# Second product of a squared-ReLU FFN with the token rows stationary, and an earlier first chunk

## The chip, the cores and the metric

The kernel runs on one core of a Trainium2 chip. The core has TensorE (PE: matrix products, with its weight loads shown apart as PEld), VectorE (DVE), ScalarE (ACT), GpSimd (POOL) and SyncE (SP, which here only issues DMAs). The metric is the device time of one execution in microseconds. The kernel before takes 222.59 us (median of three runs, 222.51 to 223.92).

## The reference

Attention with sketched quadratic features, and then a feed-forward layer with squared ReLU. Batch 4, 4 heads, 1088 positions of 32 numbers each, sketches of 8 rows, so 64 features; the FFN has width 128 and 2048 hidden units, and 4352 rows pass through it.

```python
def phi(x):
    a = np.einsum('rd,bhsd->bhsr', S1, x)
    b = np.einsum('rd,bhsd->bhsr', S2, x)
    return np.einsum('bhsi,bhsj->bhsij', a, b).reshape(*x.shape[:-1], r * r)
q_p, k_p = (phi(q), phi(k))
kv = np.einsum('bhsf,bhsd->bhfd', k_p, v)
z = np.sum(k_p, axis=2)
num = np.einsum('bhsf,bhfd->bhsd', q_p, kv)
den = np.einsum('bhsf,bhf->bhs', q_p, z)[..., None] + 1e-06
attn = num / den
x = attn.transpose(0, 2, 1, 3).reshape(B * S, H * D)
h = np.maximum(x @ w_in, 0.0)
out = h * h @ w_out
```

Inputs and output are float32.

## The kernel before

**Tiles.** The 1088 positions of a batch are 1024, cut into two groups of 512 (four tiles of 128 tokens), and a remainder of 64; the remainders of two batches share a tile of 128 rows. The FFN works on chunks: eight of 512 tokens (two per batch) and one of 256 that holds all remainders. The FFN's input `xT` of a chunk is float16, 128 features by the chunk's tokens, scaled per token by a factor that is undone at the end (`beta`).

**Attention.** For each batch `k_gen` makes the features of k: transposes on TensorE (`xt_ps`, L194), projections (`ab_ps`, L180), outer products (L221, by VectorE in the first batch and GpSimd later). `Kv` accumulates the products with v in PSUM (`kv_ps`, L249), and `finish` copies them to `kvbd` (L60). `q_gen` makes the features of q, transposes them (`t_ps`, L299) and calls `x_gen`: `numerators` writes `nd` (PSUM, two banks, one buffer), and `normalize` reads it with a chain of small VectorE instructions (L329 to L351), writes the scaled rows `xs` (L358, the last reader of `nd`), which TensorE transposes (`x_ps`, L370) and ScalarE copies to `xT` (L373). `normalize` is a generator with three yields, so that its caller can put other work in between.

**FFN.** A chunk has 16 blocks, one for each 128 hidden units. `first_product` multiplies the block's 128 columns of `w_in` (stationary, float16) with `xT` into `pg` (L516); ScalarE applies ReLU (`gt`, L519); VectorE squares (`g`, L520, float32). `block` adds the second product to `po` (L535), with 128 rows of `w_out` stationary and `g`'s 512 tokens moving, both float32. The first product is issued two blocks ahead (`LOOK = 2`). After 16 blocks `po` holds the output transposed: model features by tokens.

**Store.** `store_gen` copies `po` to `oT` (ScalarE, L482), transposes the four tiles of 128 tokens back on TensorE into `o_ps` (L487, a buffer of the `ms` ring), multiplies with `beta` on VectorE (`o_sb`, L493) and issues the output DMA on SP (L501). `po` has one buffer, so the next chunk's second product waits for the copy.

**Order.** The start (`start`) is laid out by hand, instruction by instruction: it makes k and the first q group of batch 0 and pushes the first chunk (`first`) and the second group's features (`second`) through. `idle_products` are float32 products of a zero tile that only keep TensorE occupied. After the start, `block` calls with attention pieces between them (`pump`, `lanes`) give the program order, and a scheduler then orders each engine's instructions.

**PSUM.** Eight banks: `ms` two, `pg` two, `po` one, `kv` one, `nd` two.

Of the kernel before, what the change touches and what calls it, by code (L numbers as in the profile page):

```python
# [8 lines left out]
F32 = mybir.dt.float32  # L9
# [3 lines left out]
def _v(t: bass.AP, off: int, free, p0: int = 0, n: int = 128):  # L13

    p = list(t.ap)[0]
    return bass.AP(
        t.tensor, t.offset + p0 * p[0] + off, [[p[0], n]] + [list(d) for d in free]
    )
# [3 lines left out]
def kernel(  # L22
# [11 lines left out]
    nc = tc.nc  # L34

    B, H, S, D = 4, 4, 1088, 32
    DFF, NC = 2048, 16
# [3 lines left out]
    VW = D + 1  # L41
# [10 lines left out]
    fpool = ctx.enter_context(tc.tile_pool(name="ffn", bufs=3))  # L52
    pspool = ctx.enter_context(
        tc.tile_pool(name="psm", bufs=2, space=bass.MemoryType.PSUM)
    )

    def evict(eng, dst, src):
        if eng is nc.scalar:
            return nc.scalar.copy(dst, src)  # L59
        return eng.tensor_copy(out=dst, in_=src)  # L60
# [59 lines left out]
    w_o = cpool.tile([128, DFF], F32)  # L120
# [12 lines left out]
    iden = cpool.tile([128, 128], F32)  # L133
# [14 lines left out]
        nc.vector.memset(_v(v_main[i], D, [[VW, H * NJ]]), 1.0)  # L148

    def idle_products(n):  # L150
        idle_ps = pspool.tile([128, 512], F32, name="idle_ps", tag="po", bufs=1)
        for i in range(n):
            nc.tensor.matmul(idle_ps[:, 0:128], zero[:, :], zero[:, :])

# [14 lines left out]
    def spread_vrem(r, eng, pin=False):  # L169
        ins = eng.tensor_copy(  # L170
            out=_v(v_rem[r], 0, [[VW, H], [1, D]]), in_=_v(v_rm[r], 0, [[D, H], [1, D]])
        )
        if pin:
            pinned(ins)
# [11 lines left out]

    def proj_t(src, g, T, eng, tag="ms"):


        n = 4 if T == 4 else 1  # L190
        w = NJ * D if T == 4 else E
        xt_ps = pspool.tile([128, 512], F32, tag=tag, bufs=2)
        for i in range(n):
            nc.tensor.transpose(  # L194
                xt_ps[:, 128 * i : 128 * i + 128],
                src[:, w * i + 128 * g : w * i + 128 * g + 128],
                iden[:, :],
            )
        xt = apool.tile([128, 512], F32, tag="xt", bufs=4)
        evict(eng, xt[:, 0 : 128 * n], xt_ps[:, 0 : 128 * n])  # L200
        return xt

    def proj(xt, T, tag, eng, outer, ps_tag="ms", m=32):

        n = 4 if T == 4 else 1
        ab_ps = pspool.tile([128, 256], F32, tag=ps_tag, bufs=2)
        for i in range(n):
            tiled(ab_ps, 64 * i, 64, xt, 128 * i, w_bd[:, :], m=m)
        ab = apool.tile([128, 256], F32, tag="ab", bufs=3)
        if T == 4:  # L210
            evict(
                eng,
                _v(ab, 0, [[16, 4], [64, 4], [1, 16]]),
                _v(ab_ps, 0, [[64, 4], [16, 4], [1, 16]]),
            )
        else:
            evict(eng, ab[:, 0:64], ab_ps[:, 0:64])
        ph = apool.tile([128, 1024], F32, tag=tag, bufs=3)
        for t0 in range(0, T, 2):
            m = min(2, T - t0)  # L220
            outer[(t0 // 2) % len(outer)].tensor_tensor(  # L221
                out=_v(ph, 256 * t0, [[64, 4 * m], [8, 8], [1, 8]]),
                in0=_v(ab, 64 * t0, [[16, 4 * m], [1, 8], [0, 8]]),
                in1=_v(ab, 64 * t0 + 8, [[16, 4 * m], [0, 8], [1, 8]]),
                op=mult,
            )
        return ph
# [9 lines left out]
    class Kv:  # L237
# [1 line left out]

        def __init__(self, b, m=32):
            self.b, self.m, self.started = b, m, set()
            self.ps = pspool.tile([128, 2 * VW], F32, name="kv_ps", tag="kv", bufs=1)

        def _add(self, ph, c0, vt, v0, p0, n, last):
            for pr in range(2):
# [47 lines left out]
    def feature_t(ph, T, pr, eng):  # L295

        t_ps = pspool.tile([128, 512], F32, tag="ms", bufs=2)
        for t in range(T):
            nc.tensor.transpose(  # L299
                t_ps[:, 128 * t : 128 * t + 128],  # L300
                ph[:, 256 * t + 128 * pr : 256 * t + 128 * pr + 128],
                iden[:, :],
            )
        sb = apool.tile([128, 512], F32, tag=f"phT{pr}")
        evict(eng, sb[:, 0 : 128 * T], t_ps[:, 0 : 128 * T])
        return sb
# [69 lines left out]
    chunks = []  # L376
# [5 lines left out]
    def x_gen(b, g, phT, m=32):  # L382
        nd = numerators(b, phT, m)
        yield 1
        xT = apool.tile([128, 512], F16, name="xT", tag="xT", bufs=3)
        beta = yield from normalize(nd, 4, xT, 0)
        chunk_of(b, g, xT, beta)
        yield 1

    def q_gen(b, g, outer, m=32):  # L390
        eng = nc.scalar
        xt = proj_t(q_sb[b], g, 4, eng)
        yield 1
        ph = proj(xt, 4, "ph_q", eng, outer, m=m)
        yield 3
        phT = []
        for pr in range(2):
            phT.append(feature_t(ph, 4, pr, eng))
            yield 1
        yield from x_gen(b, g, phT)  # L400
# [46 lines left out]
    now = [0]  # L447
    lanes = []
# [28 lines left out]
                except StopIteration:  # L477
                    lanes.remove(lane)

    def store_gen(po, nt, betas, dsts):  # L480
        oT = fpool.tile([128, 512], F32, tag="oT", bufs=2)
        nc.scalar.copy(oT[:, 0:nt], po[:, 0:nt])  # L482
        yield 1
        T = nt // 128
        o_ps = pspool.tile([128, 512], F32, tag="ms", bufs=2)
        for t in range(T):
            nc.tensor.transpose(  # L487
                o_ps[:, 128 * t : 128 * t + 128], oT[:, 128 * t : 128 * t + 128], iden[:, :]
            )
        o_sb = fpool.tile([128, 512], F32, tag="o_sb", bufs=2)  # L490
        t0 = 0
        for beta, n in betas:
            nc.vector.tensor_tensor(  # L493
                out=_v(o_sb, 128 * t0, [[128, n], [1, 128]]),
                in0=_v(o_ps, 128 * t0, [[128, n], [1, 128]]),
                in1=_v(beta, 0, [[1, n], [0, 128]]),
                op=mult,
            )
            t0 += n
        for dst, p0, n, c0, w in dsts:  # L500
            nc.sync.dma_start(dst, _v(o_sb, c0, [[1, w]], p0, n))  # L501
        yield 1

    LOOK = 2
    stream = []
# [21 lines left out]
    po = [None]  # L527

    def block():
        while len(stream) <= LOOK and first_product():  # L530
            pass
        ci, c, nt, g2 = stream.pop(0)
        if c == 0:
            po[0] = pspool.tile([128, 512], F32, name="po", tag="po", bufs=1)
        nc.tensor.matmul(  # L535
            po[0][:, 0:nt], w_o[:, 128 * c : 128 * c + 128], g2[:, 0:nt],
            start=(c == 0), stop=(c == NC - 1),
        )
        now[0] += 1
        if c == NC - 1:  # L540
            lanes.insert(0, [store_gen(po[0], nt, *chunks[ci][2:]), now[0]])


    dve, act, pool = nc.vector, nc.scalar, nc.gpsimd
# [1 line left out]
    def whole(gen):  # L546
        for _ in gen:
            pass


    def start():
        s_ps = pspool.tile([128, 16], F32, name="s_ps", tag="kv", bufs=1)
        xk = [proj_t(k_sb[0], 0, 4, act)]
        nc.tensor.transpose(s_ps[:, :], s_nat[:, :], iden[0:16, 0:16])
        for h in range(H):
            nc.vector.tensor_copy(
                out=_v(w_bd, 16 * h, [[1, 16]], 32 * h, 32),
                in_=_v(s_ps, 0, [[1, 16]], 32 * h, 32),
            )
        xk.append(proj_t(k_sb[0], 1, 4, act))  # L560
        idle_products(2)
        pk = [proj(x, 4, "ph_k", act, (dve,), "pg", m=64) for x in xk]
        idle_products(1)
        xq = proj_t(q_sb[0], 0, 4, act)
        spread_v(0, act, 0, 4)
        pq = proj(xq, 4, "ph_q", act, (dve,), "pg", m=64)
        xkr = proj_t(k_rm[0], 0, 1, act)
        spread_v(0, act, 4, 4, (0, 1))
        spread_v(0, pool, 4, 4, (2, 3))
        spread_vrem(0, pool)  # L570
        ph_krem[0] = proj(xkr, 1, "ph_kr", act, (dve,), "pg", m=64)
        kv0 = Kv(0, 64)
        kv0.tiles(pk[0], 0, range(4))
        pqT = [feature_t(pq, 4, 0, act)]
        kv0.tiles(pk[1], 1, range(4))
        pqT.append(feature_t(pq, 4, 1, act))
        kv0.finish((dve, dve))
        first = x_gen(0, 0, pqT, 64)
        next(first)
        for c in range(4):  # L580
            act.copy(
                w_in[:, 512 * c : 512 * c + 512], w_in32[:, 512 * c : 512 * c + 512]
            )
        second = q_gen(0, 1, (dve,), 64)
        next(second)
        next(first)
        next(first)
        next(second)
        idle_products(3)
        next(first)  # L590
        whole(first)
        return second

# [30 lines left out]
    for c in range(NC):  # L624
        block()
        pump(2)
# [31 lines left out]
```

## Time and profile before

| | us |
|---|---|
| median of three runs | 222.59 |
| the three runs | 222.51, 223.92, 222.59 |
| the profiled execution, whole | 223.71 |
| its span, first to last instruction | 221.9 |
| second product, PE busy (288 records) | 140.8 |
| first product, PE busy (128 records of 512 columns) | 48.2 |
| ReLU, ACT busy (144) | 81.9 |
| squaring, DVE busy (144) | 104.0 |
| `oT` copies, ACT busy (9) | 5.1 |
| `o_ps` transposes, PE busy (34) | 5.6 |

A row of the profile gives start and length in us, engine, source line, operation, the tiles written and read, and how many like instructions are merged (x4). In brackets stands how long the engine was idle before, and what it was released by. TensorE's records overlap: a matmul's record lasts longer than the time until the next one starts. A float32 product shows as two loads and two matmul records, a float32 transpose and a float16 product as one of each. The clock of TensorE is given as the granted share of full speed; it is 0.987 on average over the span.

### The profile page before, as it was taken

To read this page: it belongs to the slowest core of one execution; us is meant where nothing else is said; L and a number is where in the kernel's file an instruction comes from. 1 tells how busy PE (TensorE), PEld (TensorE's weight loads), DVE (VectorE), ACT (ScalarE), POOL (GpSimd) and SP (SyncE) were. 2 spreads that over 40 slices of the span, in tenths; PEclk is the share of its full clock that TensorE was granted. 3 is DMA by queue.
4 is the path that set the end of the run, shared out by engine and by line. 5 is a ranking of instruction groups with operands and counts; after the bars stand their busy time and mean duration, and the time that the engine had idled before them with its cause. 6 is when DMAs were issued, how large, how long until landed. Compare 5 with 4: busy or idle time off the path is not lost.

```text
span 221.9 us, 5199 instructions
## 1 busy us (share of the span) xinstructions
PE 209.4 (94%) x2153; PEld 114.3 (52%) x2153; DVE 143.0 (64%) x279; ACT 119.7 (54%) x235; POOL 43.7 (20%) x59
## 2 busy tenths in 40 slices
PE   8886999999999999999999999999999999999991
PEld 7665555444644655545544565445545454664440
DVE  2735488566686399575785467557776876677651
ACT  3664653564566563565565743656465555575541
POOL 1302055004040473004030770004000400000000
PEclk9999799999999999999999999999999999999998
DMA  6998000004500100009100000010001000100001
GB/s 172 311 318 214 9 4 3 1 0 145 192 0 0 47 3 3 3 0 304 31 0 39 11 4 3 0 47 3 0 4 47 0 4 0 47 0 21 5 0 47
DMA packets 13575, 11.35 MB, mean 51 GB/s; under 512 B 3824, under 2 KB 11760, under 8 KB 13552
## 3 DMA queue, kind: packets, MB, share of 16 engines
q1 hardware_dynamic: 12928, 10.95, 16.1%
q8 instruction: 17, 0.28, 0.5%
q10 hardware_dynamic: 624, 0.07, 0.2%
q14 instruction: 6, 0.05, 0.1%
HBM read 8.79 MB, written 2.23 MB: 50 GB/s over the span
## 4 chain that ended last, share of the span: by engine, by line
PE 83%; SPq 5%; DMA 3%; DVE 3%; ACT 3%; issue 1%; ACTq 1%; DVEq 0%
PE po L535 52%; PE pg L516 13%; PE nd L180 4%; PE t_ps L299 3%; PE xt_ps L194 3%; SPq L79 3%; PE o_ps L487 2%; PE ab_ps L180 2%; PE kv_ps L249 2%; ACT oT L482 2%; SPq L93 2%; DMA t<-in_k_dram 2%; DMA t<-in_v_dram 1%; PE x_ps L370 1%; DVE g L520 1%
## 5 line engine op out<-in xcount | busy, mean ns | idle before, releaser
L520 DVE TENSOR_TENSOR g<-gt 128x512 f32<-128x512 f32 (+1 forms) x144 | 104.0, 729 | 59.0 <-ACT gt L519 55.8
L535 PE MATMUL po<-g,w_o 128*128 128x512 f32 (+1 forms) x288 | 140.8, 575 | 0.2 <-DVE g L520 0.2
L519 ACT ACTIVATE gt<-pg 128x512 f32<-128x512 f32 (+1 forms) x144 | 81.9, 576 | 48.9 <-PE pg L516 48.4
L535 PEld LDWEIGHTS po<-g,w_o 128*128 128x128 f32 x288 | 52.2, 192 | 28.9 <-issue 9.8
L221 POOL TENSOR_TENSOR ph<-ab 128x512 f32<-128x512 f32 (+1 forms) x27 | 32.0, 1207 | 88.8 <-ACT ab L59 88.6
L516 PE MATMUL pg<-xT,w_in 128*128 128x512 f16 x128 | 48.2, 385 | 0.3 <-DMA t<-in_v_dram 0.2
L516 PEld LDWEIGHTS <-w_in 128*128 128x128 f16 x144 | 14.3, 99 | 22.0 <-issue 19.5
L59 ACT COPY sb<-t_ps 128x512 f32<-128x512 f32 (+1 forms) x20 | 10.3, 522 | 13.1 <-PE t_ps L299 13.1
L59 ACT COPY xt<-xt_ps 128x512 f32<-128x512 f32 (+1 forms) x20 | 10.5, 523 | 11.1 <-PE xt_ps L194 11.0
L180 PEld LDWEIGHTS ab_ps<-w_bd,xt 128*32 128x32 f32 (+1 forms) x476 | 8.9, 113 | 10.0 <-ACT xt L59 6.2
L180 PE MATMUL ab_ps<-w_bd,xt 128*32 128x64 f32 (+1 forms) x476 | 11.8, 223 | 1.7 <-ACT xt L59 1.7
L180 PEld LDWEIGHTS nd<-kvbd,sb 128*32 128x32 f32 (+1 forms) x512 | 8.9, 111 | 8.3 <-issue 3.8
L59 ACT COPY ab<-ab_ps 128x256 f32<-128x256 f32 (+1 forms) x20 | 6.8, 340 | 11.5 <-PE ab_ps L180 10.9
L299 PEld LDWEIGHTS t_ps<-iden,ph 128*128 128x128 f32 x68 | 8.6, 145 | 7.4 <-issue 5.3
L299 PE MATMUL t_ps<-iden,ph 128*128 128x128 f32 x68 | 11.4, 282 | 0.0
L180 PE MATMUL nd<-kvbd,sb 128*32 128x66 f32 (+1 forms) x512 | 10.8, 222 | 0.7 <-DVE kvbd L60 0.7
L364 POOL TENSOR_TENSOR beta<-mp 128x4 f32<-128x4 f32 (+1 forms) x10 | 3.2, 324 | 38.8 <-DVE mp L346 30.9
L194 PEld LDWEIGHTS xt_ps<-iden,t 128*128 128x128 f32 x52 | 6.5, 142 | 5.7 <-issue 3.3
L194 PE MATMUL xt_ps<-iden,t 128*128 128x128 f32 x52 | 8.8, 285 | 0.2
L487 PE MATMUL o_ps<-iden,oT 128*128 128x128 f32 x34 | 5.6, 286 | 2.6 <-ACT oT L482 2.6
L249 PEld LDWEIGHTS kv_ps<-v_main,ph 128*32 128x32 f32 (+1 forms) x448 | 6.1, 113 | 3.7 <-issue 2.1
L373 ACT COPY xT<-x_ps 128x512 f16<-128x512 f16 x8 | 4.7, 585 | 5.9 <-PE x_ps L370 5.9
(54 smaller groups left out, 102.8 us busy)
## 6 DMA issues: line engine op xcount, KB each, us to landing
out_dram<-o_sb SPq DMA_DIRECT2D x8, 256.0 KB, 2.0
t<-in_k_dram SPq DMA_DIRECT2D x3, 512.0 KB, 7.8
t<-in_v_dram SPq DMA_DIRECT2D x3, 512.0 KB, 5.7
t<-in_q_dram SPq DMA_DIRECT2D x3, 512.0 KB, 5.8
w_in<-in_moe_w_in_dram SPq DMA_DIRECT2D x2, 512.0 KB, 5.6
k_sb<-in_k_dram SPq DMA_DIRECT2D x2, 256.0 KB, 3.2
q_sb<-in_q_dram SPq DMA_DIRECT2D x2, 256.0 KB, 5.4
v_sb<-in_v_dram SPq DMA_DIRECT2D x2, 256.0 KB, 5.2
```

Of the source, the lines that this page charges most:

```text
L59: return nc.scalar.copy(dst, src)
L79: return nc.sync.dma_start(_v(t, D * j0, [[NJ * D, H], [1, w * D]]), rows(src, b, 0, 128, NJ, w, j0))
L180: nc.tensor.matmul(out_ps[p0 + c : p0 + c + m, c0 : c0 + w], lhsT[:, l0 + c : l0 + c + m], rhs,)
L194: nc.tensor.transpose(xt_ps[:, 128 * i : 128 * i + 128], src[:, w * i + 128 * g : w * i + 128 * g + 128], iden[:, :],)
L221: outer[(t0 // 2) % len(outer)].tensor_tensor(out=_v(ph, 256 * t0, [[64, 4 * m], [8, 8], [1, 8]]), in0=_v(ab, 64 * t0, [[16, 4 * m], [1, 8 ...
L249: nc.tensor.matmul(self.ps[c : c + self.m, VW * pr : VW * pr + VW], _v(ph, c0 + 128 * pr + c, [[1, self.m]], p0, n), _v(vt, v0 + VW * (2 * ...
L299: nc.tensor.transpose(t_ps[:, 128 * t : 128 * t + 128], ph[:, 256 * t + 128 * pr : 256 * t + 128 * pr + 128], iden[:, :],)
L487: nc.tensor.transpose(o_ps[:, 128 * t : 128 * t + 128], oT[:, 128 * t : 128 * t + 128], iden[:, :])
L516: nc.tensor.matmul(pg[:, 0:nt], w_in[:, 128 * c : 128 * c + 128], xT[:, 0:nt])
L519: nc.scalar.activation(gt[:, 0:nt], pg[:, 0:nt], Relu)
L520: nc.vector.tensor_tensor(out=g2[:, 0:nt], in0=gt[:, 0:nt], in1=gt[:, 0:nt], op=mult)
L535: nc.tensor.matmul(po[0][:, 0:nt], w_o[:, 128 * c : 128 * c + 128], g2[:, 0:nt], start=(c == 0), stop=(c == NC - 1),)
```

## The change

1. The second product swaps its operands: for each tile of 128 tokens, `g`'s 128 columns are stationary and the 128 columns of `w_out`'s block move. A full block has four products of 128 columns in place of one of 512; `po` then holds tokens by features.
2. `store` replaces `store_gen`: no copy to `oT`, no transposes; VectorE multiplies `po` itself with `beta`, and the DMA follows. It is called directly after the chunk's last block instead of as a lane.
3. `po` gets two buffers. The bank comes from `kv`: `Kv` now takes its accumulator from the ring `nd`, with its one buffer, which `numerators` also uses. In the start, `s_ps` and the first `Kv` take theirs from the ring `po`.
4. In the start, the first chunk's whole `normalize` up to `xs` is issued ahead of the second group's projection and outer products; three idle products now come before that projection and four after it, in place of three after it.

```diff
-        idle_ps = pspool.tile([128, 512], F32, name="idle_ps", tag="po", bufs=1)
+        idle_ps = pspool.tile([128, 512], F32, name="idle_ps", tag="po", bufs=2)
...
-        def __init__(self, b, m=32):
+        def __init__(self, b, m=32, tag="nd", bufs=1):
             self.b, self.m, self.started = b, m, set()
-            self.ps = pspool.tile([128, 2 * VW], F32, name="kv_ps", tag="kv", bufs=1)
+            self.ps = pspool.tile([128, 2 * VW], F32, name="kv_ps", tag=tag, bufs=bufs)
...
-    def store_gen(po, nt, betas, dsts):
-        oT = fpool.tile([128, 512], F32, tag="oT", bufs=2)
-        nc.scalar.copy(oT[:, 0:nt], po[:, 0:nt])
-        yield 1
-        T = nt // 128
-        o_ps = pspool.tile([128, 512], F32, tag="ms", bufs=2)
-        for t in range(T):
-            nc.tensor.transpose(
-                o_ps[:, 128 * t : 128 * t + 128], oT[:, 128 * t : 128 * t + 128], iden[:, :]
-            )
+    def store(po, betas, dsts):
+
         o_sb = fpool.tile([128, 512], F32, tag="o_sb", bufs=2)
         t0 = 0
         for beta, n in betas:
             nc.vector.tensor_tensor(
                 out=_v(o_sb, 128 * t0, [[128, n], [1, 128]]),
-                in0=_v(o_ps, 128 * t0, [[128, n], [1, 128]]),
+                in0=_v(po, 128 * t0, [[128, n], [1, 128]]),
                 in1=_v(beta, 0, [[1, n], [0, 128]]),
                 op=mult,
             )
...
-            po[0] = pspool.tile([128, 512], F32, name="po", tag="po", bufs=1)
-        nc.tensor.matmul(
-            po[0][:, 0:nt], w_o[:, 128 * c : 128 * c + 128], g2[:, 0:nt],
-            start=(c == 0), stop=(c == NC - 1),
-        )
+            po[0] = pspool.tile([128, 512], F32, name="po", tag="po", bufs=2)
+
+
+        for t in range(nt // 128):
+            nc.tensor.matmul(
+                po[0][:, 128 * t : 128 * t + 128],
+                g2[:, 128 * t : 128 * t + 128],
+                w_o[:, 128 * c : 128 * c + 128],
+                start=(c == 0 and t == 0), stop=(c == NC - 1),
+                skip_group_check=True,
+            )
         now[0] += 1
         if c == NC - 1:
-            lanes.insert(0, [store_gen(po[0], nt, *chunks[ci][2:]), now[0]])
+            store(po[0], *chunks[ci][2:])
...
-        s_ps = pspool.tile([128, 16], F32, name="s_ps", tag="kv", bufs=1)
+        s_ps = pspool.tile([128, 16], F32, name="s_ps", tag="po", bufs=2)
...
-        kv0 = Kv(0, 64)
+        kv0 = Kv(0, 64, "po", 2)
...
+        for _ in range(3):
+            next(first)
         second = q_gen(0, 1, (dve,), 64)
         next(second)
-        next(first)
-        next(first)
+        idle_products(3)
         next(second)
-        idle_products(3)
-        next(first)
+        idle_products(4)
         whole(first)
```

## The prediction

> **What bounds the kernel now.** I read the page first: the engines' shares, the chain of waits and the costliest groups.
>
> ```profile
> PE 209.4 (94%) x2153; PEld 114.3 (52%) x2153; DVE 143.0 (64%) x279; ACT 119.7 (54%) x235; POOL 43.7 (20%) x59
> PE po L535 52%; PE pg L516 13%; PE nd L180 4%; PE t_ps L299 3%; PE xt_ps L194 3%; SPq L79 3%; PE o_ps L487 2%; PE ab_ps L180 2%; PE kv_ps L249 2%; ACT oT L482 2%; SPq L93 2%; DMA t<-in_k_dram 2%; DMA t<-in_v_dram 1%; PE x_ps L370 1%; DVE g L520 1%
> L535 PE MATMUL po<-g,w_o 128*128 128x512 f32 (+1 forms) x288 | 140.8, 575 | 0.2 <-DVE g L520 0.2
> L535 PEld LDWEIGHTS po<-g,w_o 128*128 128x128 f32 x288 | 52.2, 192 | 28.9 <-issue 9.8
> ```
>
> TensorE carries the chain from about 20 us to the end, and the second product (L535) is half of it. Its 288 records are two for each of 144 float32 products (128 of 512 columns, 16 of 256). PE waits 0.2 us for g in all of them, so VectorE and ScalarE have room, and every nanosecond added to a product lengthens the span. By the groups by form, 9.5 us of the loads' 28.9 idle are waits for g, without PE noticing.
>
> Next, the timeline of ordinary blocks, and of the idle products, which have exactly the new form: float32, 128x128 stationary, 128 columns moving.
>
> ```profile
> 100.59 0.39 PE L516 MATMUL pg<-xT,w_in 128*128 128x512 f16 x1
> 100.82 1.02 PE L535 MATMUL po<-g,w_o 128*128 128x512 f32 x2
> 101.68 0.38 PE L516 MATMUL pg<-xT,w_in 128*128 128x512 f16 x1
> L153 PE MATMUL idle_ps<-zero x24: 275/399/581, 1.1 to 18.2; 128*128 128x128 f32 x24
> 5.50 0.61 PE L153 MATMUL idle_ps<-zero 128*128 128x128 f32 x4
> 17.56 0.94 PE L153 MATMUL idle_ps<-zero 128*128 128x128 f32 x6
> ```
>
> Records overlap, so cadence counts, not duration. A po record lasts 0.59 us (one that stands alone in the timeline, at 99.48); two span 1.02, so they start 0.43 apart (0.429 by their exact starts). From pg to the next pg is 1.07 to 1.09. Four idle records span 0.61, each 0.275: (0.61 - 0.275) / 3 = 0.1117 us apart, about 0.1115.
>
> **Second product: a cost.** A full block goes from two records at 0.429 (0.858 us) to four products, eight records at 0.1115 (0.892): +0.034. Times 128: +4.35. A half chunk's block goes from 2 x 0.216 to 4 x 0.1115: +0.014, times 16: +0.2. Sum **+4.6 us**, all on PE, which nothing hides. Bounds: 0, if the old product is cut in four for nothing (0.858 / 8 = 0.107 per record; no gain, since as many columns stream); at the other end stands the head of the six idle records, where the load was not ahead: (0.94 - 0.275) - 5 x 0.1115 = 0.107 us, a load that shows. I take 0 of these heads per block, because the first load of a po already starts beside pg, whose 0.216 us covers it, and inside the product each load runs beside the record before it (the idle rows keep 0.1115 with just this).
>
> The Trainium skill, "TensorE: Matmul & The Clock Gate", section "Back-to-back issue gap", speaks against this change: it gives a sustained spacing of about 81 ns for 128 moving columns and 131 ns for 512, so four short matmuls would cost 324 against 131. Here the po record, with 0.429 us for 512 columns, and the idle record, with 0.1115 for 128, stand close to four to one. By the page's pair, a record taken as two such matmuls, a block would grow by 16 x 0.081 - 4 x 0.131 = 0.77 us, an estimate, and the kernel by some 100.
>
> **Store without transposes: a gain.** At the end of a chunk PE now waits for ScalarE's copy of po, then transposes:
>
> ```profile
> 48.15 0.59 PE L516 MATMUL pg<-xT,w_in 128*128 128x512 f16 x2
> 48.35 0.58 ACT L482 COPY oT<-po 128x512 f32<-128x512 f32 x1 [0.26 <-PE po L535]
> 48.99 0.66 PE L487 MATMUL o_ps<-iden,oT 128*128 128x128 f32 x4 [0.24 <-ACT oT L482]
> 49.48 1.02 PE L535 MATMUL po<-g,w_o 128*128 128x512 f32 x2
> 216.69 0.58 ACT L482 COPY oT<-po 128x512 f32<-128x512 f32 x1 [1.98 <-PE po L535]
> 218.08 0.69 DVE L493 TENSOR_TENSOR o_sb<-o_ps,beta 128x512 f32<-128x512 f32 x1 [2.64 <-PE o_ps L487]
> ```
>
> Two pg take 2 x 0.216, so po could have gone on at 48.58; it does at 49.48: 0.90 lost, 0.41 of it waiting for oT (po has one buffer) and 0.49 in transposes. Six boundaries look like this (5.4). The one into the half chunk (o_ps at 189.5) loses 1.1, the one out of it 0.2 of waiting and 0.22 for two transposes. Middle: 6.9. At the very end the scaling could start where the copy does, at 216.69 instead of 218.08: 1.39. Sum **-8.3 us**. It needs po's second buffer, which the change gives. VectorE's scaling (0.69) reads po instead of o_ps; in the changed program's order it stands behind two squarings of the next chunk, so it delays nobody that PE waits for. The output DMA on SP follows it as before. Should the scaling of po hold up g, PE has two blocks (2.1 us) of g in hand.
>
> **kv shares nd's banks: a new wait.** The second po buffer is paid for by the kv bank: kv accumulates in nd's single buffer, and so after the xs (L358) that last reads nd. Queued behind a waiting kv on PE is everything, the next po first. In the old trace (batch 3: start of kv, then xs; batch 2: nd, kv, xs):
>
> ```profile
> 132.53 0.77 PE L249 MATMUL kv_ps<-v_main,ph 128*32 128x33 f32 x64
> 135.26 0.68 DVE L358 TENSOR_TENSOR xs<-nd,small 128x512 f16<-128x512 f32 x1
> 82.92 1.14 PE L180 MATMUL nd<-kvbd,sb 128*32 128x66 f32 x64
> 86.75 0.76 PE L249 MATMUL kv_ps<-v_main,ph 128*32 128x33 f32 x64
> 87.64 0.69 DVE L358 TENSOR_TENSOR xs<-nd,small 128x512 f16<-128x512 f32 x1
> ```
>
> Batch 1's kv (35.66) comes 1.9 us after its xs: no wait. If kv kept its place, batch 2 would wait 88.33 - 86.75 = 1.6 and batch 3 135.94 - 132.53 = 3.4: **5.0 at most**. But the changed program puts kv later: in both cases three blocks and a pg (in batch 3 a first po product too) stand between nd and kv. nd 1.07 + 3 x 1.11 + 0.22 and some 0.4 of small products and switches puts PE at kv 5.0 to 5.1 us after nd's start. xs ends 5.4 after it with two squarings in between (82.92 to 88.33), which is the new VectorE order, and 6.1 with three (106.97 to 113.04). So 0.4 to 1.0 each; I take 0.5 each, less 0.2 since kv is now one group and switches PE's tiling less often: **+0.8**, ends 0 and 5.0.
>
> **Start.** Now VectorE makes the two outer products (18.13 to 19.42) ahead of the first xs (to 20.02), though xs could follow L351 at 17.8, and PE stands still for it:
>
> ```profile
> 18.13 1.29 DVE L221 TENSOR_TENSOR ph<-ab 128x512 f32<-128x512 f32 x2 [0.36 <-ACT ab L59]
> 20.08 0.40 PE L370 MATMUL x_ps<-iden,xs 128*128 128x128 f16 x4 [1.58 <-DVE xs L358]
> 18.40:21.78 3.38, 1.57 (x13) 1.10 (x13) 1.62 (x3) 1.26 (x3) 1.22 (x4) 1.00 0.78 186
> 21.78:25.19 3.41, 3.41 (x11) 2.21 (x10) 1.99 (x3) 2.53 (x5) 0.20 (x1) 0.50 0.16 25
> ```
>
> The last two are windows (length, then PE, PEld, DVE, ACT, POOL busy, granted clock): after 3.4 us with PE busy 1.57, the clock is 0.50 for the next 3.4. With xs first it ends near 18.5, x_ps starts 1.5 us sooner (behind the four idle products: 17.6 + 8 x 0.1115). The outer products end at 19.8 instead of 19.4; their transposes wait for that, but beside x_ps, its 0.58 copy and the first pg, which wait for the copy anyway. The three idle products that are moved ahead of ab fill the 0.67 us in which PE waits for xt: nothing to 0.1. w_out landed at 17.06, k of batch 1 at 18.66: neither is late. Then: first pg at 18.6 + 1.07 (the old distance) = 19.65, gt from 20.05, g from 20.7, first po at 21.45, two of them to 23.2; the old kernel has the same work and three transposes (0.33) more behind it at 26.18, so 26.18 - 23.55: **-2.6**, of which 1.5 is xs and 1.1 the half clock. I bound it by 1.0 (xs partly eaten, clock as before) and 3.6. The latter holds if PE's share of that window rises to about 2.4 of 3.4; the window 8.13 to 11.54 had 2.44 and kept full clock. The skill's same page, section "Why this matters for your kernels", asks only for no PE pause above some 3 us; here the longest pause was 1.58 and the clock still fell, so the measurement decides.
>
> **Sum.** The profiled execution took 223.71 (span 221.9, 1.8 around it): 223.71 + 4.6 - 8.3 + 0.8 - 2.6 = 218.2. It is 1.1 above the median of 222.59, about what the half clock costs; if the median run lacked that, 222.59 + 4.6 - 8.3 + 0.8 - 1.5 = 218.2 as well. I forecast **218.2 us**.
>
> **Rivals.**
> 1. The loads of g show (slower): g changes with each product, so one load head of 0.107 per block, 144 times, is +15.4: 233.6. For it: loads already wait for g 9.5 us. Against: PE lost 0.2. It turns the sign from 31 ns per block on (4.4 / 144), a third of a head. Chance 0.14.
> 2. kv waits out the normalization (5.0 in place of 0.8), or another wait of that size eats the boundary gain: 222.4; with part of it 220.4 to 222.4. Chance 0.15.
> 3. The half clock falls elsewhere in the start: 219.3, inside the forecast's range. Chance 0.1.
> 4. More is gained than counted (kv free, fewer switches): 216.2 and below. Chance 0.05.
>
> **Numbers.** The forecast's case, with a kv wait of 0 to 2 and 1 us of play in the start, is 216.3 to 220.3: chance 0.56, with rival 3 0.66. The range goes up through rival 2 to 222.4 and leaves out rival 1 and rival 4. 1% is 2.2 us, about what can be told from no change: faster (below 220.4) 0.56 + 0.1 + 0.05 = 0.71, less 0.03 for the edge; within, rival 2 less 0.01, plus the edge: 0.17; slower, rival 1 and that 0.01: 0.15.
>
> **What would show it.** po records 0.110 to 0.113 apart, pg to pg 1.11 (right) or 1.2 and more (rival 1); no PE gap at a chunk's end and 1.4 less between the last product and the last scaling; a PE wait of VectorE's xs ahead of kv of 0.3 to 1.0 in batches 2 and 3; x_ps near 18.6 and no 0.50 clock after it. A PE idle time over 3 us in kv's groups, or a VectorE that PE waits for at each boundary, would make the forecast wrong.

## The result and the profile after

| | us | ratio to the kernel before, 95% interval |
|---|---|---|
| forecast | 218.2 (216.3 to 222.4) | |
| changed kernel, median of 4 runs | 220.25 | 0.9876 (0.9827 to 0.9926) |
| the same, measured again, median of 10 runs | 221.13 | 0.9922 (0.9891 to 0.9953) |
| best variant that still computes everything (kv accumulates in the ring `po`) | 216.9 | 0.9716 (0.9677 to 0.9754) |

The kernel before took 222.76 and 223.0 us beside the first two. The change is faster by about 1%: by 2.5 us in one measurement and 1.9 in the other, where the forecast had 4.4. The profiled execution of the changed kernel took 223.66 us (span 221.9) and is longer than its other runs; part of that is a half clock that is read below, so a second execution (222.13, span 220.3) is set beside it wherever sizes matter.

The page of the changed kernel: engines' shares, the queue that carries instructions (packets, MB, share), and the two groups of the second product.

```profile
PE 210.9 (95%) x2927; PEld 193.5 (87%) x2927; DVE 144.1 (65%) x279; ACT 115.7 (52%) x226; POOL 45.0 (20%) x59
q8 instruction: 23, 0.38, 0.7%
L529 PEld LDWEIGHTS po<-w_o,g 128*128 128x128 f32 x1088 | 142.7, 193 | 10.0 <-DVE g L511 3.1
L529 PE MATMUL po<-w_o,g 128*128 128x128 f32 x1088 | 146.0, 277 | 2.4 <-issue 1.9
```

The second product is now 1088 records instead of 288. The loads still wait for g, and PE still does not notice: its idle time of 2.4 us is of another kind, "issue", time in which the profile shows nothing that PE waited for. The q8 line had 17 packets and 0.28 MB before; it becomes important below.

The timeline of ordinary blocks, of the boundary between two chunks (the second po row belongs to the next chunk), and of the end:

```profile
45.44 0.38 PE L507 MATMUL pg<-xT,w_in 128*128 128x512 f16 x1
45.66 1.05 PE L529 MATMUL po<-w_o,g 128*128 128x128 f32 x8
46.55 0.38 PE L507 MATMUL pg<-xT,w_in 128*128 128x512 f16 x1
...
47.66 0.38 PE L507 MATMUL pg<-xT,w_in 128*128 128x512 f16 x1
47.87 1.05 PE L529 MATMUL po<-w_o,g 128*128 128x128 f32 x8
48.21 0.68 DVE L485 TENSOR_TENSOR o_sb<-po,beta 128x512 f32<-128x512 f32 x1
48.76 0.60 PE L194 MATMUL xt_ps<-iden,t 128*128 128x128 f32 x4
49.20 0.38 PE L507 MATMUL pg<-xT,w_in 128*128 128x512 f16 x1
...
215.07 2.84 PE L529 MATMUL po<-w_o,g 128*128 128x128 f32 x24
218.01 0.69 DVE L485 TENSOR_TENSOR o_sb<-po,beta 128x512 f32<-128x512 f32 x1 [1.41 <-PE po L529]
```

pg to pg is 1.11 us, and eight records span 1.05, (1.05 - 0.277) / 7 = 0.110 apart. Over the boundary PE runs on: o_sb (48.21) is made beside the next chunk's first po. At the end the scaling starts 0.1 us after the last product (215.07 + 2.84 = 217.91). These are two of the forecast's gains, and they are there.

The third, the earlier xs, is smaller than forecast in both executions of the changed kernel. `x_ps` was to start near 18.6 us; in the kernel before it starts at 20.08. Here it is in the changed kernel, in its second execution, and in the variant kv_in_po_ring that is described below:

```profile
19.98 0.39 PE L370 MATMUL x_ps<-iden,xs 128*128 128x128 f16 x4
21.02 0.39 PE L370 MATMUL x_ps<-iden,xs 128*128 128x128 f16 x4
18.21 0.39 PE L370 MATMUL x_ps<-iden,xs 128*128 128x128 f16 x4
```

The same timeline around kv and nd, where they were given back:

```profile
86.36 0.38 PE L507 MATMUL pg<-xT,w_in 128*128 128x512 f16 x1
87.05 1.29 PE L249 MATMUL kv_ps<-v_main,ph 128*32 128x33 f32 x128 [0.30 <-DVE xs L358]
88.26 0.60 PE L529 MATMUL po<-w_o,g 128*128 128x128 f32 x3
90.78 0.71 PE L529 MATMUL po<-w_o,g 128*128 128x128 f32 x5 [1.92 <-issue]
...
142.15 0.31 PE L180 MATMUL nd<-kvbd,sb 128*32 128x66 f32 x4 [1.00 <-issue]
```

The wait for xs (0.30) is there, and after it two stops that nothing in the forecast stands for: one block's eight po records broken after three, 1.92 us, and 1.00 us in the middle of nd in batch 3. The profile names no engine and no buffer for either. In the second execution the stops stand at the same records and last 1.43 and 0.79. The kernel before has one such stop, a small one. The first stop of the second execution, and the one of the kernel before:

```profile
91.14 0.72 PE L529 MATMUL po<-w_o,g 128*128 128x128 f32 x5 [1.43 <-issue]
135.12 0.55 PE L249 MATMUL kv_ps<-v_main,ph 128*32 128x33 f32 x39 [0.31 <-issue]
```

### The profile page after: what moved, and what is told of

Same layout as the page of the kernel before. It is cut to its first block, busy times and chain, and to the rows that moved or that the text cites. A ratio compares the mean times of both kernels' runs of the same rounds, so it can differ in the third digit from the quotient of the medians.

```text
span 221.9 us, 6730 instructions
## 1 busy us (share of the span) xinstructions
PE 210.9 (95%) x2927; PEld 193.5 (87%) x2927; DVE 144.1 (65%) x279; ACT 115.7 (52%) x226; POOL 45.0 (20%) x59
## 4 chain that ended last, share of the span: by engine, by line
PE 81%; DVE 10%; issue 2%; ACT 1%; DVEq 0%
PE po L529 50%; PE pg L507 12%; PE nd L180 4%; DVE g L511 4%; PE t_ps L299 3%; PE ab_ps L180 3%; PE kv_ps L249 3%; PE xt_ps L194 3%; DVE xs L358 1%; DVE small L334 1%; PE x_ps L370 1%; PE idle_ps L153 1%; DVE mp L346 1%; DVE small L339 1%; ACT gt L510 1%
## 5 line engine op out<-in xcount | busy, mean ns | idle before, releaser
L529 PEld LDWEIGHTS po<-w_o,g 128*128 128x128 f32 x1088 | 142.7, 193 | 10.0 <-DVE g L511 3.1
L529 PE MATMUL po<-w_o,g 128*128 128x128 f32 x1088 | 146.0, 277 | 2.4 <-issue 1.9
L511 DVE TENSOR_TENSOR g<-gt 128x512 f32<-128x512 f32 (+1 forms) x144 | 106.2, 747 | 52.5 <-ACT gt L510 50.6
L507 PE MATMUL pg<-xT,w_in 128*128 128x512 f16 x128 | 48.9, 383 | 0.4 <-ACT xT L373 0.3
L364 POOL TENSOR_TENSOR beta<-mp 128x4 f32<-128x4 f32 (+1 forms) x10 | 4.3, 433 | 49.5 <-DVE mp L346 49.3
L299 PEld LDWEIGHTS t_ps<-iden,ph 128*128 128x128 f32 x68 | 8.0, 142 | 0.4
L153 PE MATMUL idle_ps<-zero 128*128 128x128 f32 x32 | 6.5, 359 | 1.1 <-DVE warm L136 1.1
L221 DVE TENSOR_TENSOR ph<-ab 128x512 f32<-128x512 f32 (+1 forms) x9 | 5.6, 677 | 2.4 <-ACT ab L59 2.3
L485 DVE TENSOR_TENSOR o_sb<-po,beta 128x512 f32<-128x512 f32 (+1 forms) x10 | 6.1, 605 | 1.5 <-PE po L529 1.4
```

The costliest lines, as they stand in the source:

```text
L221: outer[(t0 // 2) % len(outer)].tensor_tensor(out=_v(ph, 256 * t0, [[64, 4 * m], [8, 8], [1, 8]]), in0=_v(ab, 64 * t0, [[16, 4 * m], [1, 8 ...
L299: nc.tensor.transpose(t_ps[:, 128 * t : 128 * t + 128], ph[:, 256 * t + 128 * pr : 256 * t + 128 * pr + 128], iden[:, :],)
L485: nc.vector.tensor_tensor(out=_v(o_sb, 128 * t0, [[128, n], [1, 128]]), in0=_v(po, 128 * t0, [[128, n], [1, 128]]), in1=_v(beta, 0, [[1, n ...
L507: nc.tensor.matmul(pg[:, 0:nt], w_in[:, 128 * c : 128 * c + 128], xT[:, 0:nt])
L511: nc.vector.tensor_tensor(out=g2[:, 0:nt], in0=gt[:, 0:nt], in1=gt[:, 0:nt], op=mult)
L529: nc.tensor.matmul(po[0][:, 128 * t : 128 * t + 128], g2[:, 128 * t : 128 * t + 128], w_o[:, 128 * c : 128 * c + 128], start=(c == 0 and t ...
```

## The experiments

Theory when the first ones were chosen: the 2 us that are missing are these stops, which come with kv in one group behind the single nd buffer. Rivals: the product costs more than 4.6; the new start gives less; the half clock falls elsewhere. The theory became sharper in three steps.

**First step: each part alone.**

*kv_in_po_ring.* On the changed kernel, kv's accumulator moves from nd's single buffer to po's two.

```diff
-        def __init__(self, b, m=32, tag="nd", bufs=1):
+        def __init__(self, b, m=32, tag="po", bufs=2):
```

> The changed kernel, with every kv accumulator in po's two-buffer ring instead of nd's single buffer; nothing else. In the program's order kv then stands again in two groups of 32 products and one of 8 with blocks between, as before the change. Theory A (instruction supply): in the changed kernel's profile PE stands still 1.92 us and 1.00 us for nothing that the profile shows, right behind the 64 kv products in one go (256 records in 1.2 us), because its instructions come in pieces of 16 KB (23 fetches for 5887 PE and PEld records, about 256 each) and a group eats one faster than the next arrives. Then splitting the group removes both stops (at most 0.4 left in all), and the wait of kv for xs (0.47 in batch 2) goes too: 217 us, 2.5 to 3.5 below the changed kernel's 220.25. Rival B: the stops come from the extra records of the four-way product wherever they stand; then they move elsewhere and only the 0.5 is won: about 219.7. Rival C: kv in po's ring makes a chunk's first po product wait for kv's copies; then over 220.3.

Measured: 216.9 us, 0.9716 (0.9677 to 0.9754). Its timeline in batch 2:

```profile
83.38 0.77 PE L249 MATMUL kv_ps<-v_main,ph 128*32 128x33 f32 x64
84.08 0.39 PE L507 MATMUL pg<-xT,w_in 128*128 128x512 f16 x1
84.30 1.05 PE L529 MATMUL po<-w_o,g 128*128 128x128 f32 x8
85.29 0.77 PE L249 MATMUL kv_ps<-v_main,ph 128*32 128x33 f32 x64
```

kv no longer waits, comes in two groups with a block between them, and there is no stop anywhere. This is 3.3 us below the changed kernel's 220.25, and the first execution had 0.30 + 1.92 + 1.00 = 3.2 of wait and stops. So kv's place decides; whether by its wait, its bunching or its luck is open.

*old_product.* On the changed kernel, the one product of 512 columns comes back. The store still reads po without transposes, so the transposes of the result are left out.

```diff
-        for t in range(nt // 128):
-            nc.tensor.matmul(
-                po[0][:, 128 * t : 128 * t + 128],
-                g2[:, 128 * t : 128 * t + 128],
-                w_o[:, 128 * c : 128 * c + 128],
...
+        nc.tensor.matmul(
+            po[0][:, 0:nt], w_o[:, 128 * c : 128 * c + 128], g2[:, 0:nt],
+            start=(c == 0), stop=(c == NC - 1),
+        )
```

> The changed kernel with the second product in its old form (w_out stationary, 512 columns of g moving), all else as changed; po then holds features by tokens, and the transposes are left out, so the output is not the reference's. It prices the swap of operands alone. By the prediction's step the swap costs 4.6 us: block cadence pg to pg 1.074 instead of 1.108. Theory A: kv still stands in one group of 64 and 8, so a stop without a shown cause of 0.5 to 2 us in batch 2 or 3 stays, though there are fewer records around it; 215 to 216 us. Rival B (extra records are the cause): no stop over 0.3 us; 214 us or less.

Measured: 213.19 us, 0.9536 (0.9493 to 0.958). From the start of the first po to the end of the last this execution takes 186.62 us with one stop of 1.76, kv_in_po_ring 189.80 with none: the swap costs 189.80 - (186.62 - 1.76) = 4.94 us, against 4.6. (The two also differ in kv's place; by shift_148 below that is worth some 0.2.) That leaves little room for load heads. The stop is the surprise, because PE has only 4254 records here, against 5854: more instructions in all are not the cause.

```profile
84.29 1.27 PE L249 MATMUL kv_ps<-v_main,ph 128*32 128x33 f32 x125
87.31 0.25 PE L249 MATMUL kv_ps<-v_main,ph 128*32 128x33 f32 x3 [1.76 <-issue]
```

It breaks kv three records before its end, where in the changed kernel it broke the po behind it.

*old_start* is the changed kernel with the old order in `start`, and *new_start_only* the kernel before with the new order; old_start and new_start_only in turn:

```diff
-        for _ in range(3):
-            next(first)
         second = q_gen(0, 1, (dve,), 64)
         next(second)
-        idle_products(3)
+        next(first)
+        next(first)
         next(second)
-        idle_products(4)
+        idle_products(3)
+        next(first)
```

```diff
+        for _ in range(3):
+            next(first)
         second = q_gen(0, 1, (dve,), 64)
         next(second)
-        next(first)
-        next(first)
-        next(second)
         idle_products(3)
-        next(first)
+        next(second)
+        idle_products(4)
```

> The changed kernel with the start in the order of before (outer products of the second group ahead of the first chunk's xs, three idle products). It prices the new start: by the prediction's step 1.5 us of earlier xs, and 1.1 more where the half clock falls behind the pause: 221.8 to 222.9. If the new start brings nothing because its stop behind the first ab products (0.34 us without a shown cause) and the later outer products eat it: 220.3.

> The kernel of before with only the new order of the start; product, store and PSUM rings as before. By the prediction's step 1.5 to 2.6 us less than before: 220.0 to 221.2, with x_ps about 1.5 us earlier and no half clock in the 3.4 us after it. If the start's gain needs the other parts, or is eaten by waits behind it: 222 or more.

Measured: old_start 220.47, 0.9868 (0.9834 to 0.9902), only 0.2 above the changed kernel; new_start_only 221.22, 0.9908 (0.9876 to 0.994), 1.8 below the kernel before. The two disagree on what the start is worth. The trace of old_start shows why it is a bad subtraction: its stops are shorter (0.81 and 0.31, at 90.49 and 139.74), and no half clock follows its start.

**Second step: the start without stops, kv bunched alone, the boundary alone.**

*after_again* is the changed kernel, unchanged, for the second execution and ten runs. *po_ring_old_start* is kv_in_po_ring with the start of old_start. *before_kv_at_once* takes only the bunching into the kernel before: the two groups of kv are issued without a block between them.

```diff
+        yield 1
         kv = Kv(b)
         for g in range(2):
             kv.tiles(phs[g], g, range(4))
-            yield 1
         kv.finish((nc.vector, nc.vector))
```

*two_po_old_product* is the kernel before with the new start, two po buffers, and kv and `s_ps` in po's ring: old product, old transposes.

```diff
-            self.ps = pspool.tile([128, 2 * VW], F32, name="kv_ps", tag="kv", bufs=1)
+            self.ps = pspool.tile([128, 2 * VW], F32, name="kv_ps", tag="po", bufs=2)
...
-            po[0] = pspool.tile([128, 512], F32, name="po", tag="po", bufs=1)
+            po[0] = pspool.tile([128, 512], F32, name="po", tag="po", bufs=2)
```

> The changed kernel, unchanged, beside the others on one chip: its first profile had the two stops behind kv (2.9 us) and 3.4 us of half clock in them, its other runs were 2.7 to 4.2 us shorter. Theory A (instruction supply): stops without a shown cause stand again behind the 64 kv products of batches 2 and 3, of 0.3 to 2 us each; 219.4 to 221. If they were an accident of that one run: none over 0.3 us, and the time still near 220.

> The changed kernel with kv in po's ring (as in the run before of that name, 216.9 us) and the old order of the start. It prices the new start where no stop stands behind kv. By the prediction's step 1.5 us, more where the half clock falls in: 218.4 to 219.5. If the start is worth as little as the run with the old start alone showed (0.2): 217.1.

> The kernel of before with one thing: k_gen issues kv's 64 products and the 8 of the remainder in one go, without the blocks between; kv keeps its own bank, so it waits for no xs, and there is no extra record. Theory A: stops without a shown cause of 0.5 to 2 us appear behind kv in one or more of batches 1 to 3, against 0.31 in all before; fewer switches of the array's tiling give back about 0.2 per batch; 223 to 225 us. Rival B (extra records) and a cause in nd's bank: no stop over 0.3; 222.0 to 222.6.

> The kernel of before with its product and its store with copy and transposes, but with two po buffers, kv in po's ring, and the new start. It tells the second buffer from the swap of operands. If the boundary's gain is the wait for oT (0.41 six times, 0.6 and 0.2 at the half chunk: 3.3) and the swap only trades 4.6 to 5 us of records against 3.7 of transposes and 1.4 at the end: 223 - 1.8 - 3.3 = 217.9, within 1.2 of the changed kernel with kv in po's ring (216.9). If the swap is worth more than that: 219 or above.

Measured:
- after_again: 221.13, 0.9922 (0.9891 to 0.9953). Stops of 1.43 and 0.79 at the same two records as before, and again 0.30 for xs in batch 2 and none in batch 3.
- po_ring_old_start: 219.1, 0.9823 (0.9784 to 0.9862), no stop. Against kv_in_po_ring's 216.9 the new start is worth 2.2 us.
- before_kv_at_once: 223.16, 1.0003 (0.9978 to 1.0029). One stop of 0.51 in batch 3, none in batch 2. Bunching by itself is not enough; the expectation is met at its lower edge at most.
- two_po_old_product: 219.11, 0.981 (0.9763 to 0.9856), 1.2 above its expectation; its profile has a stop of 0.49 in the start and 0.77 of waiting for VectorE at 169.62, neither of them foreseen. The boundary no longer waits for `oT`. So some 2 us of gain over new_start_only (221.22, in another comparison) need no swap of operands. kv_in_po_ring is another 2.2 us faster, but 1.3 of that lies ahead of its first po (21.07 against 22.37 us); from there to the end its execution takes 193.73 us against 194.65, and the wait of 0.77 is most of the difference. The swap, which costs 4.9, gains little more than that by the transposes and the later end that it removes.

What sorts all stops came out here. PE's records, loads included, were counted in order. Every stop, in every kernel, stands 165 to 185 records past a multiple of 256, with other work under it each time: po, kv, nd, ab. q8's packets carry 0.38 MB / 23 = 16.5 KB each, and 5854 / 23 is 254 records for one packet; in the kernel before it is 4306 / 17 = 253. So q8 fetches PE's instructions, 256 at a time. The fetches keep step with PE: in all 14 traces the n-th begins while PE is between 42 records ahead of record 256 (n - 1) + 174 and 248 past it. Kv's 64 products in one go (128 matmul records and as many loads) are 256 records in 1.3 us, a whole packet.

**Third step: shift the count.** If that is so, tiny products at the start of the program, which change nothing in the later order, must move the stops. *shift_148* replaces three of the first six idle products by 40 tiny ones; *shift_32* replaces one by nine, in the same way; each float32 product counts four records (two loads, two matmuls), so the count moves by 160 - 12 = 148 and 36 - 4 = 32; *po_ring_shift_148* does the first on kv_in_po_ring.

```diff
-    idle_products(6)
+    idle_products(3)
+    tiny_ps = pspool.tile([128, 512], F32, name="tiny_ps", tag="po", bufs=2)
+    for i in range(40):
+        c = 32 * (i % 4)
+        nc.tensor.matmul(tiny_ps[c : c + 32, 0:64], zero[:, c : c + 32], zero[:, 0:64])
```

*kv_64_columns* halves the number of kv's products on the changed kernel (in `k_gen`):

```diff
-        kv = Kv(b)
+        kv = Kv(b, 64)
```

> The changed kernel with three of the six first idle products replaced by 40 tiny ones (32 columns stationary, 64 moving): the rest of PE's stream is the same, but starts 148 records later (160 more, 12 fewer). Theory A, refined: in every trace so far PE's stops without a shown cause in the blocks fell 170 to 182 records after a multiple of 256, 2.3 to 2.7 us after a fetch of 16 KB of instructions had begun; the fetch is asked for when a piece of 256 is done, arrives some 3.7 us later, and PE stops if it has eaten the next piece before. With the stream shifted by 148, the 256 records between two such edges around the kv groups take over 3.7 us in each batch: no stop over 0.3, and 2 us less than the changed kernel's 220.3 to 221.1: 218 to 219. Rival (the stop belongs to kv behind nd's bank, whatever the record numbers): the stops stay where they are, behind kv of batches 2 and 3, and so does the time, 220 to 221.5.

> As the run with the shift of 148, but one idle product replaced by 9 tiny ones: a shift of 32 records. Theory A, refined: the stop in batch 2 shrinks below 0.8 us and the one in batch 3 grows to 1.5 to 2.5 (the edge moves to the front of its kv group), one in batch 1 of up to 1 may appear; the sum stays near that of the changed kernel: 219.8 to 221.5. Rival (place, not record number): batch 2's stop stays the larger one, 1.4 to 1.9 against 0.8 to 1.0.

> The changed kernel with kv in po's ring (216.9 us, no stop) and the same shift of 148 records. It tells whether that version is only lucky in its record numbers. Theory A, refined: a kv group there holds 128 records, so at most one stop of up to 1 us in batch 3 (nd and kv stand next to each other, 256 records in a row); 216.5 to 218. If kv in po's ring is free of stops for another reason: none at all, 216.5 to 217.2.

> The changed kernel with kv of batches 1 to 3 in products of 64 stationary columns instead of 32, as its first batch has: half the records (128 + 16 instead of 256 + 32 in a batch), still in one group behind nd's bank, with the wait for xs. In the old trace 32 records of 64 columns took 1.08 us for four tiles against 0.77 for 64 of 32 columns: some 0.3 us more for four tiles, six times, 1.5 to 2 us. Theory A: no stop over 0.3, so 2 to 2.9 less and 1.5 to 2 more: 219.5 to 220.5. Rival (place): the stops stay and the longer products add to them: 222 or more.

Measured:
- shift_148: 218.35, 0.9764 (0.9734 to 0.9795). No stop is left; the wait for xs is:

```profile
86.15 1.29 PE L253 MATMUL kv_ps<-v_main,ph 128*32 128x33 f32 x128 [0.30 <-DVE xs L362]
87.37 1.16 PE L533 MATMUL po<-w_o,g 128*128 128x128 f32 x8
```

  From the first po to the end this execution takes 193.88 us, kv_in_po_ring 193.73: once the stops are gone, kv behind nd's single buffer costs no more than its wait of 0.30.

- shift_32: 221.72, 0.9905 (0.9867 to 0.9943). The stop of batch 2 is gone, that of batch 3 is larger and has moved into kv:

```profile
134.20 1.29 PE L253 MATMUL kv_ps<-v_main,ph 128*32 128x33 f32 x128
135.42 0.31 PE L253 MATMUL kv_ps<-v_rem,ph 64*32 64x33 f32 x10
137.66 0.26 PE L253 MATMUL kv_ps<-v_rem,ph 64*32 64x33 f32 x6 [1.94 <-issue]
```

- po_ring_shift_148: 218.97, 0.9786 (0.9752 to 0.982), 1.0 above the upper end expected. One stop of 0.48 in batch 3. So kv_in_po_ring's own count is a lucky one, though by less than the 2.1 us between the two times. Its execution is 2.34 us longer, and 1.66 of that lies ahead of the first po (22.73 against 21.07), where the tiny products stand and the clock was first granted in full at 6.11 us instead of 4.08. Behind it are the stop of 0.48 and 0.2 more.
- kv_64_columns: 220.1, 0.9829 (0.9779 to 0.9878). No stop, but the group lasts 2.06 instead of 1.29 us, three times: the cure costs what it saves.

```profile
86.47 2.06 PE L249 MATMUL kv_ps<-v_main,ph 128*64 128x33 f32 x64 [0.30 <-DVE xs L358]
```

The table is worked out from the traces. It sets the n-th fetch of a trace beside the edge at record 256 n + 174 (each stop lies within ten records of it) and gives how long after that fetch began PE arrives at the edge, and how long it stops there (us). The 14 traces have 275 such pairs; these are the shortest arrivals, and two longer ones.

```
kernel               record  arrives after fetch began   stop   sum
shift_32              4270            0.41               1.94   2.34
old_product           2222            0.61               1.76   2.38
changed kernel        2734            0.70               1.92   2.62
after_again           2734            1.01               1.43   2.44
old_start             2734            1.53               0.81   2.34
after_again           4270            1.55               0.79   2.33
changed kernel        4270            1.65               1.00   2.65
po_ring_shift_148     4270            1.88               0.48   2.36
before_kv_at_once     3246            1.91               0.51   2.43
old_start             4270            1.97               0.31   2.27
kernel before         3246            2.07               0.31   2.38
shift_32               430            2.24               none
changed kernel         430            2.26               0.23   2.49
two_po_old_product     430            2.27               0.49   2.76
po_ring_old_start      430            2.27               none
two_po_old_product    3246            2.37               none
new_start_only        3246            2.39               none
kv_in_po_ring         4014            2.50               none
po_ring_old_start     2734            2.91               none
before_kv_at_once     2222            3.24               none
```

Where PE stopped, it went on 2.27 to 2.76 us after that fetch began, whatever it was doing. Each of the 11 arrivals up to 2.07 us stops, two of the six from 2.24 to 2.39 do, and none of the 258 later ones. The Trainium skill, "Runtime: NRT & Kernel Launch", section "Instruction fetch mechanics", states the block of 16 KiB with 256 instructions, and the count here agrees (253 to 254 records for one packet). It also says that the fetch is hidden behind the issue of instructions; here it is not, with up to 1.94 us for one edge. What starts a fetch, and so why it sometimes begins after PE passed the edge before and sometimes ahead of it, no run here shows.

## Why the prediction was right or wrong

**Right in kind, 2 to 3 us too low.** The kernel is faster, for the reasons given, and the measured time lies in the range. That is partly luck: the forecast's own case ended at 220.3, which 220.25 just meets, and 221.13 lies inside only by what was allowed for rival 2, whose cause is not the one found. By parts:

- **Second product, +4.6:** measured 4.94. The cadence that was read from the idle products holds (pg to pg 1.11). Rival 1, a load head in each block, is out: it would have been 15 us, and PE's row names 2.4 us of idle time in all, 1.9 of it "issue". The pair of spacings from the skill's page that would have made it some 100 us is contradicted by the 0.110.
- **Store, -8.3:** po_ring_old_start against the kernel before has the swap and the store, the same start, and no stop but the 0.31 of the kernel before: 219.1 - 223.0 = -3.9, less 4.94 is -8.8, or -8.5 without that stop. The stretch from the first po to the end agrees: kv_in_po_ring's 193.73 us against new_start_only's 197.37, both without a stop there, is -3.64, less 4.94 is -8.6. Both halves are visible at 47.87 and 218.01.
- **Start, -2.6:** -1.8 alone (new_start_only), -2.2 without stops. The earlier xs is confirmed in kind: from the first `ab_ps` product to x_ps it is 14.0 us in the kernel before and 12.5 in seven kernels with the new start, which is the 1.5 forecast. In the two executions of the changed kernel it is 13.1 and 13.4, so the forecast's 18.6 was missed. In the first, 0.5 is lost at record 439, where PE stops for 0.23 at an edge of the fetch; in the second, 0.8 is lost before 9.6 us, and the clock was first granted in full at 9.66. The half clock is not a fixed price: old_start has the same 1.58 us pause and none. So the term is a little too large, by what its second half was counted for. Rival 3 did not occur.
- **kv in nd's bank, +0.8: the step that failed.** The wait for xs was put at 0.5 in each of two batches; it is a gap of 0.30 in batch 2 and nothing in batch 3. But "kv is now one group and switches PE's tiling less often" was booked as a gain of 0.2, and that one group is the cost: it runs through a whole packet of instructions in 1.3 us. With the stops the term is 0.30 + 1.92 + 1.00 = 3.2 in the first execution and 0.30 + 1.43 + 0.79 = 2.5 in the second, against 0.8. The row that could have warned was in the trace of the kernel before: a stop of 0.31 with "issue" as its releaser, at 135.12 (shown above) and record 3241, inside the second group of kv in batch 3, where nd and both groups come within 4 us.

Put together: 222.8 + 4.94 - 8.8 - 2.0 + 2.5 to 3.2 = 219.4 to 220.1, against 220.25 and 221.13. What is left, 0.1 to 1.7 us, fits a start that brought less than the 2.0: the first po comes at 23.05 and 23.88 us in the changed kernel's two executions, at 21.07 in kv_in_po_ring and at 23.72 in the kernel before. How its other runs started is not on record, so this part stays open. Without the stops the changed kernel takes 218.35 beside 223.63 (shift_148), a gain of 5.3 where the forecast had 222.59 - 218.2 = 4.4 against the median. Rival 2 had the right size for "another wait of that size eats the boundary gain; with part of it 220.4 to 222.4", but named the normalization, which the trace acquits with 0.30.

The forecast's own mark, "a PE idle time over 3 us in kv's groups", was not reached in one place, but 2.5 to 3.2 in sum around them.

## What to carry to other kernels

Where an edit puts many small products next to each other, count instructions as well as time. Of the 20 places in these traces where PE ran through the 256 records (loads included) between two edges of the fetch in 3.2 us or less, 11 have a stop; of the 255 slower ones only two do, both in the start. No dependence shows there, so leave long instructions, here a block of the FFN, between groups of short ones. An idle time on a saturated engine that the profile ascribes to "issue" is worth explaining before an edit that shortens the instructions around it. When a buffer is taken from one user, ask how the program's order changes with it: the same second po buffer, shared with kv instead of withheld from it, keeps kv in two groups with a block between them and gives 216.9 us in place of 220.25, the best of the kernels here that compute everything, though its count of records is a favourable one (218.97 with another).

## What the hardware showed that was not expected

**The clock falls by the share of fixed windows, not by the length of a pause.** In all traces the full clock begins and ends at whole multiples of 3.413 us from where it was first granted (kernel before: 4.71 to 21.78 is five of them). So the windows can be laid out from the first change of the clock. The columns are the window, its length, the busy time and instructions of PE, PEld, DVE, ACT and POOL, the granted clock, the DMA share and GB/s. The changed kernel, after its stop of 1.92:

```profile
89.03:92.43 3.40, 1.65 (x27) 1.46 (x27) 0.45 (x2) 0.31 (x1) 0.00 (x0) 1.00 0.02 5
92.43:95.84 3.41, 3.41 (x20) 3.20 (x20) 1.39 (x2) 1.37 (x3) 0.00 (x0) 0.50 0.00 0
```

Its second execution, after 1.43:

```profile
88.16:91.57 3.41, 1.98 (x126) 1.85 (x113) 0.98 (x3) 0.05 (x1) 0.00 (x0) 1.00 0.02 5
91.57:94.98 3.41, 3.41 (x45) 3.15 (x44) 1.42 (x4) 1.92 (x5) 0.00 (x0) 1.00 0.02 5
```

And old_start, whose pause of 1.58 is cut in two by the border at 19.77:

```profile
16.36:19.77 3.41, 1.96 (x26) 1.46 (x24) 2.85 (x10) 1.31 (x3) 0.20 (x1) 1.00 1.12 304
19.77:23.18 3.41, 2.37 (x18) 1.78 (x19) 1.24 (x3) 2.17 (x5) 1.43 (x4) 1.00 0.52 113
```

Between the start and the last products, each window with PE busy 1.83 us or less (1.60, 1.60, 1.61, 1.65, 1.83 in five kernels) is followed by a window at half clock, and none with 1.96 or more is; near the end of the program two windows of 1.66 and 1.70 were not, which is open. In the kernel before, the pause of the start lies in one window (18.37 to 21.78, PE busy 1.60). So whether a pause costs half a clock for 3.4 us depends on where the windows lie, and this changes from run to run. The Trainium skill, "TensorE: Matmul & The Clock Gate", section "What's actually happening", has the free-running window of 3413 ns, with which these traces agree; as the condition for a fall it names an idle window, and in this case a window with PE busy for half of it was enough.
